# Feed-forward blocks of 2, 2, 4, 4, 4 token tiles instead of 2, 3, 4, 4, 3, and groups of six chunk pairs in the blocks of two

## Chip, cores, metric

The kernel runs on one core of a Trainium2 chip. The metric is the device time in microseconds (us). The engines are PE (TensorE, matmuls), PEld (its weight loads), DVE (VectorE), ACT (ScalarE), POOL (GpSimd) and SP (which issues the DMAs).

## The reference

One transformer layer on 2048 tokens of width 576: a conditioned layer norm, linear attention with 32 heads whose feature maps are softmaxes, a residual, a second conditioned layer norm, and a feed-forward of width 4608, all in bf16. What matters here is the end:

```python
h = _layernorm(x) * (1 + ca) + sa
x = x + ga * attention(h)                 # q, k, v, feature maps, numerator / denominator, @ wo
h = _layernorm(x) * (1 + cb) + sb
x = x + gb * (relu(h @ w1) @ w2)          # w1: 576 x 4608, w2: 4608 x 576
```

## The kernel before

The 16 tiles of 128 tokens go through the feed-forward in blocks. A block's first layer keeps its tokens as the moving operand (`nn` = 128 columns for each tile in the block) and w1 as the weights. There are 36 chunks of 128 hidden units. The input has 576 rows = 4 x 128 + 64, so each chunk takes four full matmuls and one "half chunk" of 64 rows; chunks j and j + 18 make a pair, whose two half chunks sit in the upper and lower 64 rows of the array and run at the same time. Chunk pairs are taken in groups: the group's first pairs get their full matmuls, then all pairs of the group get their half chunks, then the later pairs get their full ones. A matmul writes to a PSUM bank (512 fp32 columns); there are eight: four `psf`, `num0` to `num2`, and `pt`.

While block b is on PE, the next block's tiles are prepared in between: the softmax numerator of attention (`num`, made from phi, the feature map of q), its transpose, the output projection (`wo_tile`, with residual and statistics), the normalised xn, and xn's transpose into `h2T`. In block 0 the transposes are PE's; later they go through HBM by DMA. `put(us, f)` gives the point of the block, in us of feed-forward work, at which a step is emitted.

```python
FB = [(0, 2), (2, 3), (5, 4), (9, 4), (13, 3)]          # first tile, tiles
QREST = (2, 4, 8, 12, 16)                               # when phi of tiles 3..7 is made, in block 0
...
def ffn(b, steps):
    per = 512 // nn                                     # 2 for two tiles: two chunks share a bank
    def full(j, hps, last): ...                         # 4 matmuls of 128 rows for each of j, j + 18
    def rest(j, hps, last): ...                         # 1 matmul of 64 rows for each of j, j + 18
    size = 4
    for j0 in range(0, NJ // 2, size):
        js = list(range(j0, min(j0 + size, NJ // 2)))
        early, later = js[:len(js) // 2], js[len(js) // 2:]
        for j in early:
            pace(8 * nn / 2400)                         # emits the steps that are due
            bank[j] = bank[j - 1] if per > 1 and j - 1 in bank else [psf(), psf()]
            full(j, part(j), False)
        ...                                             # banks for the later pairs
        for j in js:
            rest(j, part(j), j in early)
        ...                                             # relu(early); full and relu for each later pair
    for tt in range(nt): ...                            # second layer: 72 matmuls of 288 columns a tile
...
total = FB[b][1] * (18 * 9 * P / 2400 + 72 * 0.12)      # 17.3 us for each tile of block b
lead, hop = (20, 12) if by_dma else (LEAD0, 8.3)        # by_dma = b > 0, LEAD0 = 11
gap = min(7.5 if b else GAP0, (total - lead) / nt)      # GAP0 = 5, nt = tiles of block b + 1
us0 = total - lead - gap * nt                           # tile i: num at us0 + gap*i, wo_tile hop later
```

The softmax here doesn't subtract the row's maximum and nothing guards it: scores larger than these inputs give would overflow.

## Time and profile before

| | before |
|---|---|
| time, median of the first 6 runs | 415.93 us (414.54 to 417.58) |
| profiled span | 414.7 us |
| PE busy | 98% |
| feed-forward part, first matmul of block 0 to the end | 89.72 to 414.69: 324.97 us |

From the page of the kernel before: span, PE's row, the granted clock in tenths over 40 slices, and the chain that ended last by engine and by line.

```profile
span 414.7 us, 8210 instructions
...
PE 405.8 (98%) x3447; PEld 284.2 (69%) x3459; DVE 224.8 (54%) x523; ACT 136.7 (33%) x305; POOL 61.8 (15%) x76
...
PEclk9999999999999999999999999999999999999999
...
PE 91%; DVE 4%; DMA 2%; ACT 1%; issue 1%; POOLq 0%; SPq 0%; ACTq 0%
PE psf L941 32%; PE psf L880 18%; PE two L484 10%; PE psf L484 4%; PE pt L880 3%; PE psf L887 3%; DVE R_sb L520 1%; PE kvacc L546 1%; DMA rW_60<-in_A_wqkv_dram 1%; DMA ph_66<-q_hbm 1%; DVE st L387 1%; PE two L680 1%; PE one L312 1%; DMA q_hbm<-Eq 1%; DVE mv L432 0%
```

PE has work nearly all the time, the clock is full, and the chain is 91% PE. So the time is the length of PE's stream, and a change can only win by shortening that stream or closing its holes.

The timeline of PE in the kernel before: start, length, engine, line, operation, operands, count. L880 is a full matmul, L887 a half chunk, L941 the second layer. The first rows are a group of block 0 (256 columns), the last two the step from block 1 to block 2.

```profile
92.36 0.61 PE L887 MATMUL psf<-h2T,rW_59 64*128 64x256 bf16 x8
92.90 3.67 PE L880 MATMUL psf<-h2T,rW_59 128*128 128x256 bf16 x32
96.50 0.61 PE L887 MATMUL psf<-h2T,rW_59 64*128 64x256 bf16 x8
97.04 3.67 PE L880 MATMUL psf<-h2T,rW_59 128*128 128x256 bf16 x32
...
193.89 1.27 PE L941 MATMUL psf<-rR_65,rH_1610 128*128 128x288 bf16 x9
194.99 3.62 PE L880 MATMUL psf<-h2T,rW_59 128*128 128x512 bf16 x15
```

Read start to start: from 92.90 to 96.50 there are 32 full matmuls in 3.60 us, which is 32 steps of 109 ns and about 0.1 more. From 96.50 to 97.04 eight half chunks in four pairs take 0.54 us, which is four steps of 109 ns and again 0.1 more. The extra stands at the two changes of mode: in the trace's own start times the last full matmul before a half chunk is about 95 ns longer than the others, and the last half chunk before a full one 92 ns. This is the same at 384 columns (258 and 255 ns for 163) and at 512 (312 and 308 for 216). In the last two rows (nine matmuls of 122 ns from 193.89), block 2 follows block 1 without a hole.

The preparation chain of block 2 in the kernel before: SP's timeline (a store of xn to HBM, then the transposing load of h2T), then DVE's (xn of the last tile, then the scaling of h2T).

```profile
182.64 0.33 SPq L835 DMA_DIRECT2D xn_hbm_2416<-xn  x1
184.58 2.70 SPq L840 DMA_TRANSPOSE h2T<-xn_hbm_2416  x1
```

```profile
181.98 0.63 DVE L445 TENSOR_SCALAR xn<-x_sb,rs 128x64 bf16<-128x64 bf16 x2
...
189.35 1.70 DVE L842 TENSOR_SCALAR h2T<-h2T,mod_76 128x512 bf16<-128x512 bf16 x5 [2.02 <-DMA h2T<-xn_hbm_2416]
```

The load is issued at 184.58, the scaling starts 4.77 us later and is over at 191.05. PE needs h2T at 194.99: 4 us of slack.

### The profile page before, as it was taken

The page shows a single profiled execution, that of the slowest core. Times are in us where ns is not written, and L with a number is a line of the kernel's source. Part 1 is how long each engine was busy: PE and PEld are TensorE (multiplying, and loading weights), DVE is VectorE, ACT ScalarE, POOL GpSimd, SP SyncE. Part 2 cuts the span into 40 slices and gives each one's busy share as a digit, 9 for nine tenths or more (in the row PEclk, how much of TensorE's full clock was granted, in tenths as well). Part 3 has the DMA queues.
Part 4 walks back from the last instruction along what each step waited for, and adds up shares of the span by engine and source line. Part 5 has one row for each costly group of instructions (what it writes and reads, how often), then busy time and mean ns, then how long its engine had stood idle before and what let it go on. Part 6 is the DMA issues. An engine that isn't in the chain of part 4 may idle for free.

```text
span 414.7 us, 8210 instructions
## 1 busy us (share of the span) xinstructions
PE 405.8 (98%) x3447; PEld 284.2 (69%) x3459; DVE 224.8 (54%) x523; ACT 136.7 (33%) x305; POOL 61.8 (15%) x76
## 2 busy tenths in 40 slices
PE   8999999989999999999999999999999999999997
PEld 5777888858887565877444588774446778655776
DVE  3599999666755466443445674433445544333122
ACT  4488987575511343000344300002443000123000
POOL 6245466413200010000010110000111000000000
PEclk9999999999999999999999999999999999999999
DMA  8998973987530123112023343120022413000001
GB/s 228 210 230 180 358 264 161 269 318 217 148 81 16 43 64 95 48 45 66 14 58 89 87 123 63 50 70 5 10 77 61 136 47 78 16 1 2 2 14 31
DMA packets 67986, 42.21 MB, mean 102 GB/s; under 512 B 47980, under 2 KB 65260, under 8 KB 67436
## 3 DMA queue, kind: packets, MB, share of 16 engines
q1 hardware_dynamic: 67328, 41.66, 36.6%
q8 instruction: 27, 0.44, 0.4%
q10 hardware_dynamic: 620, 0.02, 0.1%
q14 instruction: 11, 0.09, 0.1%
HBM read 19.63 MB, written 10.68 MB: 73 GB/s over the span
## 4 chain that ended last, share of the span: by engine, by line
PE 91%; DVE 4%; DMA 2%; ACT 1%; issue 1%; POOLq 0%; SPq 0%; ACTq 0%
PE psf L941 32%; PE psf L880 18%; PE two L484 10%; PE psf L484 4%; PE pt L880 3%; PE psf L887 3%; DVE R_sb L520 1%; PE kvacc L546 1%; DMA rW_60<-in_A_wqkv_dram 1%; DMA ph_66<-q_hbm 1%; DVE st L387 1%; PE two L680 1%; PE one L312 1%; DMA q_hbm<-Eq 1%; DVE mv L432 0%
## 5 line engine op out<-in xcount | busy, mean ns | idle before, releaser
L941 PEld LDWEIGHTS <-rH_1610 128*128 128x128 bf16 x1188 | 113.2, 98 | 27.1
L941 PE MATMUL psf<-rW_60,rH_1610 128*128 128x288 bf16 (+2 forms) x891 | 113.2, 282 | 0.0
L880 PEld LDWEIGHTS <-rW_59 128*128 128x128 bf16 x720 | 68.1, 98 | 56.0 <-issue 8.1
L880 PE MATMUL psf<-h2T,rW_59 128*128 128x384 bf16 (+2 forms) x454 | 81.4, 327 | 1.1 <-ACT x_sb L323 0.4
L897 ACT ACTIVATE rH_1610<-psf 128x512 bf16<-128x512 f32 (+2 forms) x60 | 30.1, 545 | 106.5 <-PE psf L887 101.6
L535 POOL TENSOR_TENSOR Eq<-Eq,R_sb 128x576 bf16<-128x576 bf16 (+1 forms) x16 | 18.4, 1150 | 218.9 <-DVE R_sb L530 199.5
L946 DVE TENSOR_TENSOR rYT<-psf,gb_row 128x288 f32<-128x288 f32 (+2 forms) x33 | 14.7, 445 | 55.0 <-PE psf L941 54.9
L484 PEld LDWEIGHTS <-hTr 128*128 128x128 bf16 x360 | 34.2, 98 | 10.4 <-issue 1.1
L941 PE MATMUL psf<-rR_65,rH_1610 128*128 128x288 bf16 (+2 forms) x297 | 41.4, 282 | 0.0
L899 DVE TENSOR_SCALAR rH_1610<-psf 128x384 bf16<-128x384 f32 (+1 forms) x40 | 23.5, 616 | 29.8 <-PE psf L887 27.8
L520 DVE TENSOR_REDUCE R_sb<-Eq 128x64 f32<-128x1152 bf16 x16 | 21.6, 1348 | 21.3 <-ACT Eq L505 13.6
L484 PE MATMUL two<-rW_60,hTr 128*128 128x288 bf16 x240 | 31.9, 286 | 0.0
L958 POOL TENSOR_TENSOR rH_61<-rH_61,R_sb 128x1152 bf16<-128x1152 bf16 (+4 forms) x16 | 27.6, 1725 | 15.5 <-ACT R_sb L524 13.3
L391 ACT ACTIVATE rs<-mv,eps_t 128x1 f32<-128x1 f32 x14 | 4.1, 295 | 76.2 <-DVE mv L388 76.2
L495 ACT ACTIVATE rH_61<-two,rs 128x576 bf16<-128x576 f32 x32 | 22.0, 737 | 2.6 <-PE two L680 2.0
L818 DVE TENSOR_TENSOR x_sb<-x_sb,psf 128x288 bf16<-128x288 bf16 x28 | 12.2, 445 | 19.0 <-PE psf L484 18.9
L387 DVE BATCH_NORM_STATS2 st<-x_sb 128x6 f32<-128x288 bf16 x52 | 22.0, 447 | 0.7
L520 DVE TENSOR_REDUCE R_sb<-rH_61 128x64 f32<-128x1152 bf16 x16 | 21.4, 1340 | 0.0
L484 PE MATMUL psf<-wo_sb,oT 128*128 128x288 bf16 x140 | 19.4, 286 | 0.1
L484 PEld LDWEIGHTS <-oT 128*128 128x128 bf16 x160 | 15.6, 98 | 4.3 <-issue 0.3
L899 DVE TENSOR_SCALAR rH_1610<-pt 128x384 bf16<-128x384 f32 (+1 forms) x16 | 9.9, 621 | 12.7 <-PE pt L880 12.7
L947 DVE TENSOR_TENSOR x_sb<-rYT,x_sb 128x288 bf16<-128x288 f32 (+2 forms) x33 | 14.8, 448 | 1.0
(436 smaller groups left out, 449.9 us busy)
## 6 DMA issues: line engine op xcount, KB each, us to landing
rW_59<-in_B_w_dram SPq DMA_DIRECT2D x4, 1152.0 KB, 10.1
q_hbm<-Eq SPq DMA_DIRECT2D x16, 288.0 KB, 2.1
rW_60<-in_B_w_dram SPq DMA_DIRECT2D x3, 1296.0 KB, 10.2
out_dram<-x_sb SPq DMA_DIRECT2D x15, 144.0 KB, 1.8
o_hbm<-o_sb SPq DMA_DIRECT2D x11, 160.0 KB, 1.8
rW_60<-in_w_mod_dram SPq DMA_DIRECT2D x3, 576.0 KB
rR_65<-in_B_w_dram SPq DMA_DIRECT2D x1, 1296.0 KB, 6.8
rW_59<-in_w_mod_dram SPq DMA_DIRECT2D x4, 288.0 KB, 3.5
```

Source lines behind the costliest of these rows:

```text
L387: nc.vector.bn_stats(out=s[:, hf, :], in_=x_sb[:, t, hf * HD2:(hf + 1) * HD2])
L484: nc.tensor.matmul(ps(bk)[:, 0:cn], lhsT=lhs(ci), rhs=rhs[:, ci, c0:c0 + cn], start=(first and ci == CO[0]), stop=(ci == CO[-1]))
L495: nc.scalar.activation(out=E[:, :, sgn, :].rearrange("p (b h) e -> p b h e", b=2), in_=ps[:, :, 0:HD2].rearrange("p b (h e) -> p b h e", e ...
L520: nc.vector.tensor_reduce(out=R[:, 0, :], in_=flat.rearrange("p (n e) -> p n e", e=DH), axis=AXX, op=ALU.add)
L535: eng.tensor_tensor(out=e, in0=e, in1=R[:, 1, h0:h1].unsqueeze(2).to_broadcast([P, h1 - h0, DH]), op=ALU.mult)
L880: nc.tensor.matmul(ps, lhsT=w1a[:, ci, jj * P:(jj + 1) * P], rhs=hb[:, ci, :], start=(not last and ci == 0 and first(j)), stop=(last and c ...
L897: nc.scalar.activation(out=o, in_=i_, func=ACT.Relu)
L899: nc.vector.tensor_relu(o, i_)
L941: nc.tensor.matmul(ps[:, 0:cn], lhsT=H1[:, j, tt * P:(tt + 1) * P], rhs=w2q[j // 9][:, j % 9, c0:c0 + cn], start=(j == 0), stop=(j == NJ - 1))
L946: nc.vector.tensor_tensor(out=y, in0=ps[:, 0:cn], in1=gb_row[:, c0:c0 + cn], op=ALU.mult)
L947: nc.vector.tensor_tensor(out=x_sb[:, t, c0:c0 + cn], in0=y, in1=x_sb[:, t, c0:c0 + cn], op=ALU.add)
L958: eng.tensor_tensor(out=e, in0=e, in1=R[:, 1, n0:n1].unsqueeze(2).to_broadcast([P, n1 - n0, DH]), op=ALU.mult)
```

## The change

Its intent: fuller PSUM banks and fewer groups. The blocks become 2, 2, 4, 4, 4 tiles. In blocks of two tiles, six chunk pairs (three pairs of banks) form a group, so the half chunks of twelve chunks stand end to end, and there are three groups instead of five (4, 4, 4, 4, 2 pairs). The times of the q work in block 0 move too.

```diff
-QREST = (2, 4, 8, 12, 16)
+QREST = (2, 6, 9.5, 15, 20)
-    FB = [(0, 2), (2, 3), (5, 4), (9, 4), (13, 3)]
+    FB = [(0, 2), (2, 2), (4, 4), (8, 4), (12, 4)]
...
-        size = 4
+        size = 6 if per > 1 else 4
-            early, later = js[:len(js) // 2], js[len(js) // 2:]
+            early, later = js[:2 if per > 1 else len(js) // 2], js[2 if per > 1 else len(js) // 2:]
...
-                if few:
-                    bank[j] = bank[j - 1] if per > 1 and i else [psf(), psf()]
+                if per > 1:
+                    bank[j] = bank[j - 1] if i % 2 else [pn.tile([P, 512], FP32, name="num2"), one_b()] if i == 0 else [psf(), psf()]
+                elif few:
+                    bank[j] = [psf(), psf()]
...
-                    pace(10 * nn / 2400, few)
+                    pace(10 * nn / 2400, few and (per == 1 or j > later[1]))
...
-                steps.append((us, lambda: f(*args), f in (num_tile, q_tile)))
+                steps.append((us, lambda: f(*args), f in ((num_tile, q_tile) if FB[b][1] > 2 else (tr_tile,))))
...
-                    put(QREST[i], q_rest, t, max(0, int(QREST[i] / 0.97) - 2))
+                    put(QREST[i], q_rest, t, min(NJ // 2 - 1, max(0, int(QREST[i] / 0.97) - 2)))
```

More of the change, by code (lines that the diff above doesn't have):

```diff
@@ L872, in first @@
         def first(j):
-            return per == 1 or j % 2 == 0 or j == NJ // 2 - 1
+            return per == 1 or j % 2 == 0
         def full(j, hps, last):
@@ L908, in part @@
             def part(j):
-                m = (j % 2) * nn if per > 1 and len(js) == 4 else 0
+                m = (j % 2) * nn if per > 1 else 0
                 return [ps[:, m:m + nn] for ps in bank[j]]
@@ L925, in ffn @@
                 rest(j, part(j), j in early)
-            group = lambda l: [l] if per > 1 else [[j] for j in l]
+            group = lambda l: [l[i:i + 2] for i in range(0, len(l), 2)] if per > 1 else [[j] for j in l]
             for g in group(early):
```

## The prediction

> **What bounds the kernel now.** TensorE's stream of matmuls. The page gives PE busy 98%, granted clock 1.00, and the chain that ended last as 91% PE. In the timeline of PE the feed-forward part (89.7 us to the end) has hardly a hole: start to start, matmuls of 256, 288, 384 and 512 columns take 109, 122, 163 and 216 ns, which is N/2.4 plus about 2.5 ns[...]. Beyond that I find in that part only:
> - 25 passes through the half chunks of rows (64-row matmuls, two at once). Each costs about 95 ns going in and 92 ns coming out, whatever the width: 0.19 us a pass, 4.7 us in all. The Trainium skill (TensorEngine Tiling, Key Properties) says that changing the tiling mode drains TensorE; the trace agrees.
> - some five short waits (for PSUM banks or phi), about 1 us in all, and 0.8 us at the start of the first block.
>
> **What the change does.**
> 1. Widths 256, 384, 512, 512, 384 become 256, 256, 512, 512, 512. There are still five blocks with the same number of matmuls, and the sum of columns is the same. As the cost is linear in N, this is worth 0.
> 2. Blocks of two tiles take three groups of six chunk pairs instead of five of four (the last of two). Passes: 25 become 3+3+5+5+5 = 21, so 4 x 0.19 = -0.75 us, all on the critical path.
> 3. Block 1 has two tiles instead of three, so one tile fewer is prepared by PE transposes during block 0: five transposes of o (0.27 us) and five of xn (0.27 us) go to DMA: -0.5 us.
> 4. New pressure: block 1 (two tiles, 35 us of feed-forward) must now prepare four tiles; the gap is 3.6 us a tile instead of 7.5. The last output projection stands about 12.5 us of feed-forward before the block's end (before: 15.5). From the trace: projection start to h2T ready = 4.3 (residual, statistics, xn) + 1.9 (store) + 4.8 (transposing DMA) + 1.7 (scale) = 12.7 us, against 1.2 + 12.5 = 13.7 us available. It just fits, with 1 us of slack where before had 4. In block 1's first layer DVE is nearly full (9 relus of 0.65, four softmax ratios of 1.4, two residual chains of 3.1): I allow 0.3 to 1 us of PE waits for PSUM banks there.
> 5. The later blocks of four have the pattern that block 2 has now, which shows no stall above 0.25 us. The tail is unchanged.
>
> Sum: -0.75 - 0.5 + about 0.4 = -0.9 us.
>
> **Prediction: 415.0 us, range 413.0 to 417.2. Faster by over 2%: 0.01; within 2%: 0.96; slower by over 2%: 0.03.**
>
> **What would show each step.** (1) The same start-to-start times, 109 and 216 ns. (2) 21 runs of 64-row matmuls; in blocks 0 and 1 three of 12, with 0.19 us of extra each. (3) 10 transposes of o and 10 of xn on PE after block 0 starts, from 15 and 15. (4) PE waiting for h2T at the start of block 2 would mean that the chain did not fit; waits on psf in block 1, bank pressure.
>
> **What would make it wrong.** The DMA chain of four tiles falling behind (two o buffers, three xn buffers), and block 2 starting late: slower by 2 to 6 us. Or six-pair groups waiting for relu before the shared banks come free in every group: up to 1 us each.

## The result

The changed kernel took 415.19 us (median of 20 runs, 413.13 to 416.11), the kernel before 416.4 us in the same rounds (40 runs). The ratio is 0.9971, 95% interval 0.9956 to 0.9985. Ratios here and below are the mean time of one kernel's fast runs over the mean of the other's fast runs of the same rounds, so not quite the ratio of the medians quoted.

From the page of the changed kernel, the same lines:

```profile
span 413.9 us, 8176 instructions
...
PE 404.3 (98%) x3433; PEld 284.3 (69%) x3449; DVE 223.1 (54%) x514; ACT 134.4 (32%) x293; POOL 61.8 (15%) x76
...
PEclk9999999999999999999999999999999999999999
...
PE 94%; DVE 3%; DMA 1%; ACT 1%; issue 0%; SPq 0%; ACTq 0%
PE psf L943 34%; PE psf L880 17%; PE two L484 10%; PE psf L484 4%; PE pt L880 4%; PE psf L887 3%; PE kvacc L546 1%; DMA rW_60<-in_A_wqkv_dram 1%; DVE R_sb L520 1%; DVE st L387 1%; PE two L680 1%; PE one L312 1%; DVE mv L432 0%; DVE rW_60 L382 0%; PE one L281 0%
```

The timeline of PE in the changed kernel: a group of block 0 with its twelve half chunks (the rows left out are four on `num` and `pt`), and the step from block 1 to block 2.

```profile
92.56 0.39 PE L887 MATMUL psf<-h2T,rW_59 64*128 64x256 bf16 x4
...
93.01 0.38 PE L887 MATMUL psf<-h2T,rW_59 64*128 64x256 bf16 x4
93.33 0.61 PE L880 MATMUL num_1629<-h2T,rW_59 128*128 128x256 bf16 x4
...
172.26 1.27 PE L943 MATMUL psf<-rR_65,rH_1610 128*128 128x288 bf16 x9
173.51 2.86 PE L880 MATMUL psf<-h2T,rW_59 128*128 128x512 bf16 x10
```

The twelve half chunks run from 92.56 to 93.33: 0.77 us, which is six pairs of 109 ns and 0.11 more (the other 0.09 is ahead of them). So the change of mode still costs the same 0.19 us, but once for twelve and not for eight. The last row is new: from 173.51, the first four matmuls of block 2 stand 323 ns apart in the trace, not 216, and 173.51 itself is 0.145 us late. PE lost 0.145 + 3 x 0.107 = 0.47 us there. (My expectations below say 0.57: I had counted one step too many, beside a matmul whose record is missing.)

The preparation chain of block 2 in the changed kernel, SP and DVE:

```profile
159.06 5.23 SPq L835 DMA_DIRECT2D xn_hbm_2380<-xn  x2
166.66 2.76 SPq L840 DMA_TRANSPOSE h2T<-xn_hbm_2380  x1
```

```profile
163.29 0.64 DVE L445 TENSOR_SCALAR xn<-x_sb,rs 128x64 bf16<-128x64 bf16 x2
...
173.05 1.70 DVE L842 TENSOR_SCALAR h2T<-h2T,mod_76 128x512 bf16<-128x512 bf16 x5 [3.43 <-DMA h2T<-xn_hbm_2380]
```

The last store is issued at 163.96 (second of the two that the first row merges), and the load only 2.70 us later (1.93 before). The scaling starts 6.39 us after the load's issue (4.77 before). PE then takes each piece of h2T as DVE delivers it, which is the 323 ns.

Because the part ahead of the feed-forward is the same program in both and yet ends anywhere from 87.9 to 89.9 us in the profiles below, I compare the feed-forward parts, block by block (from the first full matmul of a block to that of the next, PE timeline):

| profile | block 0 | 1 | 2 | 3 | 4 | sum | runs of half chunks | half clock near 90 us |
|---|---|---|---|---|---|---|---|---|
| before | 43.66 | 61.61 | 82.61 | 80.05 | 57.04 | 324.97 | 25 | no |
| changed | 41.46 | 42.13 | 82.93 | 82.60 | 74.82 | 323.94 | 21 | no |
| a1_after | 43.04 | 41.99 | 82.77 | 82.61 | 74.79 | 325.20 | 21 | yes |
| e1_lead | 41.45 | 41.99 | 82.61 | 82.61 | 74.81 | 323.47 | 21 | no |
| e2_groups4 | 41.88 | 43.30 | 82.93 | 82.60 | 74.82 | 325.53 | 25 | no |
| e3_pairs | 43.03 | 41.99 | 84.10 | 83.98 | 75.65 | 328.75 | 33 | yes |
| e4_blocks_old | 45.02 | 61.62 | 82.61 | 80.10 | 57.02 | 326.37 | 23 | no |
| e5_qrest_old | 62.53 | 41.99 | 82.91 | 82.61 | 74.81 | 344.84 | 21 | no (later, see there) |
| e6_featdma | 42.44 | 41.99 | 82.61 | 83.74 | 74.59 | 325.37 | 21 | yes |
| e7_shift | 42.61 | 41.99 | 82.63 | 82.60 | 74.79 | 324.62 | 21 | yes |
| e8_lead_fill | 41.28 | 42.03 | 82.61 | 82.60 | 74.80 | 323.32 | 21 | no |
| e9_featdma_fill | 40.72 | 42.12 | 82.61 | 82.61 | 74.59 | 322.65 | 21 | no (by its 109 ns steps; the clock record is empty) |
| e10_before_fill | 44.18 | 61.61 | 82.61 | 83.69 | 57.03 | 329.12 | 25 | no |

Before to changed is -1.03 us. The start times account for it: four runs of half chunks fewer, 4 x 0.188 = -0.75; ten PE transposes of 56 ns fewer (five of o, five of xn), -0.56; two short waits that went (0.15 and 0.27 us in blocks 1 and 3 of before), -0.42; the late h2T, +0.47; and the stretch from the start of the last matmul to the end, which is 3.13 us before and 3.46 in the changed kernel, +0.32. (It is 3.43 to 3.46 in the other kernels with the new blocks, but 3.23 in e6 and e9. The matmuls and the last store do not make it: from the last landing of that store to the end, where only event semaphores of the program's end are left, it is 0.87 us before and 1.15 in the changed kernel.) That makes -0.94; 0.1 us is not placed. Four gaps of 0.22 us, one each in blocks 2 and 3 of both traces, are no waits: a matmul's record is missing there, seven of eight being recorded. The prediction's "five short waits, about 1 us" must count such gaps, as the trace of before has only the two waits after the start of block 0.

### The profile page after: what moved, and what is told of

Same layout as the page of the kernel before. It is cut to its first block, busy times and chain, and to the rows that moved or that the text cites. A ratio compares the mean times of both kernels' runs of the same rounds, so it can differ in the third digit from the quotient of the medians.

```text
span 413.9 us, 8176 instructions
## 1 busy us (share of the span) xinstructions
PE 404.3 (98%) x3433; PEld 284.3 (69%) x3449; DVE 223.1 (54%) x514; ACT 134.4 (32%) x293; POOL 61.8 (15%) x76
## 4 chain that ended last, share of the span: by engine, by line
PE 94%; DVE 3%; DMA 1%; ACT 1%; issue 0%; SPq 0%; ACTq 0%
PE psf L943 34%; PE psf L880 17%; PE two L484 10%; PE psf L484 4%; PE pt L880 4%; PE psf L887 3%; PE kvacc L546 1%; DMA rW_60<-in_A_wqkv_dram 1%; DVE R_sb L520 1%; DVE st L387 1%; PE two L680 1%; PE one L312 1%; DVE mv L432 0%; DVE rW_60 L382 0%; PE one L281 0%
## 5 line engine op out<-in xcount | busy, mean ns | idle before, releaser
L880 PE MATMUL psf<-h2T,rW_59 128*128 128x512 bf16 (+1 forms) x420 | 77.5, 330 | 1.2 <-ACT x_sb L323 0.4
L897 ACT ACTIVATE rH_1610<-psf 128x512 bf16<-128x512 f32 x48 | 26.7, 595 | 104.6 <-PE psf L887 97.3
L899 DVE TENSOR_SCALAR rH_1610<-psf 128x512 bf16<-128x512 f32 x36 | 23.7, 681 | 27.6 <-PE psf L887 24.5
L880 PE MATMUL pt<-h2T,rW_59 128*128 128x256 bf16 (+1 forms) x96 | 19.5, 326 | 0.0
L899 DVE TENSOR_SCALAR rH_1610<-pt 128x512 bf16<-128x512 f32 x15 | 10.4, 691 | 15.2 <-PE pt L880 15.2
```

The source lines that it names most:

```text
L880: nc.tensor.matmul(ps, lhsT=w1a[:, ci, jj * P:(jj + 1) * P], rhs=hb[:, ci, :], start=(not last and ci == 0 and first(j)), stop=(last and c ...
L897: nc.scalar.activation(out=o, in_=i_, func=ACT.Relu)
L899: nc.vector.tensor_relu(o, i_)
```

## The experiments

Each was checked against the reference and timed against the kernel before on the same chip. The interval of a ratio from six runs is about 0.3% (1.2 us), wider than most of what is asked. Two theories of the late h2T stand against each other: F, an instruction fetch holds up the load; S, four tiles in a two-tile block do not fit.

### a1_after: the changed kernel again

No edit.

> The changed kernel once more, so that the variants stand beside it on one chip. All theories: ratio to the kernel before 0.996 to 0.9985 again. The question it answers is the start of block 2: in the first profile TensorE lost 0.57 us there, fed by the scaling of h2T chunk by chunk, and the two last DMAs of that chain took 2.6 us (store of xn) and 6.4 us (transposing load) where the kernel before shows 1.8 and 4.7; each overlapped an instruction-fetch packet (8 KB and 16 KB, 0.7 and 1.1 us) and one straggling stream of packets ended 0.6 and 1.4 us after the others. Theory F (the fetch is the cause): if the fetches fall at the same place again the same loss of 0.4 to 0.8 us appears; if they fall elsewhere, the load takes 4.7 us and the loss is 0 to 0.2. Theory S (the four tiles in 35 us simply do not fit): the loss is 0.5 us or more wherever the fetches fall.

Measured: 415.34 us, ratio 0.9962 (0.9934 to 0.9990). The fetches fell at the same place, and the load again took 6.38 us to the scaling; the wait at the start of block 2 was about 0.2 us. This agrees with F and does not exclude S. It also brought something unasked: block 0 took 43.04 us, 1.58 more. The stretches of this profile (busy time and count of each engine, then the granted clock, the DMA share and GB/s):

```profile
core 0: us, PE busy (x) PEld busy (x) DVE busy (x) ACT busy (x) POOL busy (x), PEclk, DMA share, GB/s
86.00:90.00 4.00, 2.52 (x22) 1.54 (x21) 3.23 (x12) 3.50 (x8) 0.64 (x1) 1.00 1.09 392
90.00:94.00 4.00, 3.64 (x25) 2.19 (x23) 0.00 (x0) 0.89 (x3) 0.00 (x0) 0.59 0.25 95
94.00:98.00 4.00, 4.00 (x38) 3.47 (x37) 1.90 (x3) 2.21 (x6) 1.35 (x2) 0.98 0.89 220
```

In the second stretch the mean clock is 0.59. The trace's clock record has half clock from 90.7 us for 3.4 us, beginning 81.9 us after the clock was first released.

### e1_lead: more lead in block 1

```diff
-            lead, hop = (20, 12) if by_dma else (LEAD0, 8.3)
+            lead, hop = (22 if b == 1 else 20, 12) if by_dma else (LEAD0, 8.3)
```

> The changed kernel with the preparation in block 1 started so that the last projection stands 1.5 us earlier (gap 3.14 us a tile instead of 3.64). Theory chain-late (TensorE waits at the start of block 2 because the chain projection, xn, store, transposing load, scale ends too late): the wait of 0.57 us at the start of block 2 is gone, first matmuls of block 2 start 216 ns apart, time 0.3 to 0.6 us below the changed kernel (ratio to before about 0.9957), if tighter spacing costs no new PSUM wait. Rival (the wait is for PSUM banks, or for the relus of block 1): the wait stays at 0.5 us or more and the time is the same as the changed kernel's.

Measured: 414.21 us, ratio 0.9946 (0.9915 to 0.9978). Blocks 1 and 2 are 41.99 and 82.61 us, the matmuls at the start of block 2 stand 216 ns apart, and no new wait came. DVE of this profile:

```profile
168.57 1.70 DVE L842 TENSOR_SCALAR h2T<-h2T,mod 128x512 bf16<-128x512 bf16 x5 [4.72 <-DMA h2T<-xn_hbm]
```

The scaling starts 2.95 us ahead of block 2's first matmul (171.52). So it was the chain's lateness that PE waited for, not banks. (This load was not held up, as the table under e7_shift shows: 4.92 us to its last completion. That the longer lead also takes a late load is seen in e8_lead_fill.) The gain on the trace is 0.47 us; on the clock it is not resolved against a1_after.

### e2_groups4: new blocks, old groups

```diff
-        size = 6 if per > 1 else 4
+        size = 4
```
and the other lines about groups and banks as in the kernel before.

> The new blocks (2, 2, 4, 4, 4) with the old groups of four pairs in the blocks of two tiles. Theory passes (each run of 64-row matmuls costs 0.19 us for going in and coming out): 25 runs in the trace instead of 21, and 0.75 us more in blocks 0 and 1 together than in the changed kernel; ratio to before about 0.9988 (0.9975 to 1.0005). Rival (the gain comes from the fuller relus and from the blocks themselves, the groups do nothing): same time as the changed kernel within 0.2 us, 0.997.

Measured: 416.26 us, ratio 0.9997 (0.9960 to 1.0034). PE in block 0:

```profile
92.54 0.61 PE L887 MATMUL psf<-h2T,rW 64*128 64x256 bf16 x8
93.08 3.67 PE L880 MATMUL psf<-h2T,rW 128*128 128x256 bf16 x32
96.68 0.61 PE L887 MATMUL psf<-h2T,rW 64*128 64x256 bf16 x8
97.22 1.05 PE L880 MATMUL psf<-h2T,rW 128*128 128x256 bf16 x8
```

Eight half chunks at a time again, 25 runs. Blocks 0 and 1 together are 85.18 us, 83.59 in the changed kernel: +1.59, twice the expected 0.75. Block 0, where nothing else differs, gives 0.42 for two runs (0.38 expected). Block 1 has besides a wait of 0.42 us (start times) of an output projection for `psf`, and PE waits 0.33 us more at its end for h2T. So the runs cost what was claimed, and the six-pair groups save a bank wait that I had not seen. In e2 the projection stands right behind the half chunks and waits for the relu of a `psf` bank; in the changed kernel it stands behind the full matmuls on `num2` and `pt` (half chunks over at 148.55, projection at 150.31), and by then the relu is done.

### e4_blocks_old: old blocks, new groups

```diff
-    FB = [(0, 2), (2, 2), (4, 4), (8, 4), (12, 4)]
+    FB = [(0, 2), (2, 3), (5, 4), (9, 4), (13, 3)]
-QREST = (2, 6, 9.5, 15, 20)
+QREST = (2, 4, 8, 12, 16)
```

> The old blocks (2, 3, 4, 4, 3) and old times of the q work, with the new groups of six pairs, which then touch block 0 alone. Theory passes: 23 runs of 64-row matmuls, block 0 shorter by 0.38 us, ratio to before about 0.9991 (0.998 to 1.0). Ten transposes of o and xn more than in the changed kernel, and no wait at the start of block 2. Rival (six-pair groups bring waits for banks): block 0 the same or longer than before.

Measured: 416.65 us, ratio 1.0003 (0.9975 to 1.0030). Two runs fewer, yet block 0 is 1.36 us longer than before. The expectation was wrong, and the rival nearer. PE's waits in block 0, who waited for whom, in total, times, longest:

```profile
PE num L769 <- DMA ph<-q_hbm: 0.8, 1, 0.8
PE pt L792 <- ACT rH L897: 0.7, 1, 0.7
```

Three tiles to prepare put the steps 5 us earlier than two do. The transpose of o then falls into the first layer and needs the bank `pt`, which the six-pair groups now use, so it waits for the relu of that bank; and the numerator of tile 3 comes before its phi has landed (it was due at 103.87 us; in the kernel before, with the same times but four-pair groups, it stands at 106.59). In start times these are 0.90 and 0.89 us, and -0.38 + 1.79 = +1.41 against 1.36 measured. The groups pay only together with the smaller block 1, which moves both steps past the first layer.

### e7_shift: instruction fetches moved

```diff
     spin(5)
+    spin(64, 1)          # 64 matmuls of one column while PE waits for its first data
     turn_m(1)
```

> The changed kernel with 64 matmuls of one column (128 instructions of TensorE with their weight loads) put in at its very start, where TensorE waits for its first data. They only move the places in time at which TensorE's 16 KB instruction fetches fall, by half of the distance between two. In the three traces so far with the same instruction stream in block 1 (both of the changed kernel, and the old groups) 15 of the 16 completions of the transposing load of block 2 came by 4.8 us and the sixteenth at 6.4 us, just behind such a fetch (4.1 to 5.2 us after the issue). Theory F (the fetch holds up one of the 16 DMA engines and with it the load): no fetch between 3.5 and 5 us after the issue, all 16 completions by 4.9 us, the wait of TensorE at the start of block 2 is at most 0.2 us (0.57 and 0.31 before). Rival S (the load is slow for another reason at that place, such as the output store beside it): 6.4 us again and the wait stays. Time from the first matmul of block 0 to the end 323.5 us if no throttled stretch falls in (323.94 in the changed kernel's first profile); total the same as the changed kernel within 1 us, as the start may come some tenths later.

Measured: 417.41 us, ratio 1.0025 (1.0000 to 1.0051). The scaling of h2T starts 4.79 us after the load's issue and blocks 1 and 2 are 41.99 and 82.63 us: the wait is gone, with the lead unchanged. DMA of the changed kernel in a window of block 1's end (packets, MB, share; then issues with size and time to landing), then that of this kernel:

```profile
q8 instruction: 1, 0.02, 0.6%
q14 instruction: 1, 0.01, 0.4%
...
h2T<-xn_hbm_2380 SPq DMA_TRANSPOSE x1, 6.4
```

```profile
q14 instruction: 1, 0.01, 0.3%
...
h2T<-xn_hbm SPq DMA_TRANSPOSE x1, 4.8
```

No q8 fetch, and a load of 4.8 instead of 6.4 us. The records of the load's 16 completions, us after its issue, in eight loads of several profiles:

```
profile, load of block   15th    16th    q8 fetch of 16 KB, from - to
before, 2                4.74    4.75    none
changed, 2               4.80    6.36    4.07 - 5.19
a1_after, 2              4.88    6.35    4.30 - 5.30
e2_groups4, 2            4.80    6.33    4.10 - 5.23
changed, 4               4.63    6.10    3.86 - 5.02
a1_after, 4              4.70    4.71    3.90 - 5.07
e1_lead, 2               4.89    4.92    4.21 - 5.42
e7_shift, 2              4.74    4.76    none
```

Fifteen completions are in time and one is 1.4 to 1.6 us late, in four loads, each beside a fetch of 16 KB; but four loads had all 16 in time, two of those beside a fetch. These eight are a choice. All 13 profiles together hold 41 such loads of h2T. In 17 of them a 16 KB fetch was in flight in the last part (later than 2 us after the issue): ten of these had one completion 1.4 to 1.6 us late, seven lost 0.12 us at most. Of the 24 others none lost more than 0.05 us. So in these traces the loss needs a fetch, but a fetch does not always bring it, and what decides stays open. A fetch is one packet of 16 KB, 0.9 to 2.3 us long; the kernel before has 27 of them for 6906 matmuls and weight loads, one for 256, so they should be PE's instructions. If such a packet goes through one DMA engine, only the load's part on that engine would be late, which fits the one late completion. The Trainium skill (DMA: Bandwidth & Descriptors, Queues, rings and completion order) says that each engine goes round its queues packet by packet; the traces agree as far as they go, but they do not name the engine of a packet, so that it was the same engine is inferred. S is refuted: with the old lead the chain fits when no fetch meets it, by 0.5 us (scaling over at 173.88, block 2 at 174.40).

The total was worse than I expected by 2 us, and that is not explained in full. All six runs have the clock of 0.996, that is the half-clock stretch of a1_after, against nine of 21 for the changed kernel; block 0 is 1.15 us longer for it. Why the rest of the start is slower was not followed.

### e3_pairs: more runs of half chunks

```diff
-        size = 6 if per > 1 else 4
+        size = 6 if per > 1 else 2
```

> The changed kernel with groups of two pairs instead of four in the three blocks of four tiles: nine runs of 64-row matmuls a block instead of five, 33 in all instead of 21. Theory passes (0.188 us a run whatever its length): the blocks of four are 0.75 us longer each, 2.26 us in all, ratio to before about 1.0024 (1.001 to 1.004); if it is more, the trace must show waits for PSUM banks beside it. Rival (a run costs by its number of matmuls or the trace's start times mislead): the time stays at that of the changed kernel, 0.997.

Measured: 418.65 us, ratio 1.0049 (1.0012 to 1.0085): slower than the kernel before, by less than 1%. PE in the last block, where no other work is mixed in:

```profile
343.49 0.60 PE L887 MATMUL psf<-h2T,rW 64*128 64x512 bf16 x4
344.03 3.63 PE L880 MATMUL psf<-h2T,rW 128*128 128x512 bf16 x16
347.59 0.61 PE L887 MATMUL psf<-h2T,rW 64*128 64x512 bf16 x4
348.13 3.63 PE L880 MATMUL psf<-h2T,rW 128*128 128x512 bf16 x16
```

Sixteen full and four half matmuls take 347.59 - 343.49 = 4.10 us; at 216 ns for each of 18 slots it would be 3.89. So 0.21 us a group, and block 4 is 0.83 us longer for four groups more. Blocks 2 and 3 are 1.5 and 1.4 us longer than in e1_lead: 0.83 for the runs and one wait each of 0.53 us (start times) of an output projection for `psf`, as the expectation allowed. This is the amplified form of e2's test, and it shows on the clock too.

### e5_qrest_old: old times of the q work

```diff
-QREST = (2, 6, 9.5, 15, 20)
+QREST = (2, 4, 8, 12, 16)
```

> The changed kernel with the old times of the q work (2, 4, 8, 12, 16). There are four phi buffers after the first two tiles; with the new blocks the softmax numerators of tiles 2 and 3 are at 13.6 and 18.6 us, so the phi of tiles 6 and 7, put at 12 and 16 us, would be written in program order into the buffers of tiles 2 and 3 before these are read. Expected: a WRONG result on purpose (tiles 2 and 3), at about the same time. Rival (the new times of the q work are a tuning for speed, not needed): correct, and slower by over 0.5 us.

Measured: correct, 436.35 us in one run of unknown state. Both halves of the expectation failed. PE's waits in block 0:

```profile
PE num L769 <- DMA ph<-q_hbm: 17.7, 2, 11.0
```

Block 0 is 62.5 us long, 41.46 in the changed kernel; the numerators of tiles 2 and 3 wait 17.7 us for phi and the clock is halved twice behind these waits. So the numerators wait for a phi that is written late, as they would if they waited for tiles 6 and 7. Why the result passed (whether the right phi was read, or the comparison does not see two tiles' phi) stays open. In either case the new times are not a fine tuning; without them the new blocks lose 20 us.

### e6_featdma: xn of block 1 transposed by DMA as well

```diff
-            lead, hop = (20, 12) if by_dma else (LEAD0, 8.3)
+            lead, hop = (22 if b == 1 else 20, 12) if by_dma else (LEAD0 + 2, 8.3)
-                if by_dma:
+                if True:
                     put(us + hop + 0.1, xn_out, b + 1, t0 + i)
-            if by_dma:
+            if True:
                 put(total - 6, feat_dma, b + 1)
```

> The changed kernel with the longer lead in block 1 (as in e1_lead) and with the features of block 1 transposed by DMA instead of TensorE in block 0, which starts that preparation 2 us earlier. Theory (TensorE's stream is all that counts): ten transposes of xn fewer, 0.55 us, so block 0 is 40.9 us long instead of 41.45, the feed-forward part about 322.9 us, ratio to before about 0.994 to 0.995. Rival (the chain through HBM does not fit into block 0, which also carries the q work and the last weights on the same queue): TensorE waits at the start of block 1 or for phi of tile 3 in block 0, and block 0 is not shorter than 41.45 us.

Measured: 414.53 us, ratio 0.9959 (0.9929 to 0.9989). Block 0 was 42.44 us, with the half-clock stretch in it, so this profile alone could not tell. Block 3 lost 1.1 us:

```profile
PE num L769 <- DMA ph<-q_hbm: 1.0, 1, 1.0
```

The store ahead of that phi had 15 completions by 2.05 us and the sixteenth at 4.28, with a 16 KB fetch from 301.79 to 303.33 us on the way (store issued at 300.61). In e1_lead the same store's sixteenth came at 2.73. This is F's pattern at another place.

### e10_before_fill, e8_lead_fill, e9_featdma_fill: holes ahead of block 0 filled

Half clock near 90 us stands in four of the first ten profiles (a1, e3, e6, e7); the five that the expectation below speaks of counted the half clock of e5, which has another origin.

```diff
-    ... Qm6 J1a J1b Je1a:v
+    ... Qm6 HT5 J1a J1b HT1 Je1a:v
+        elif name == "HT":
+            fill = acc()                                  # a PSUM bank pair that is free here
+            for i in range(n):
+                nc.tensor.matmul(fill[:, 0, :], lhsT=ident[:, :], rhs=wo_sb[:, 0, 0:512], start=True, stop=True)
```

> The kernel before with six dummy matmuls of 512 columns (results never read) in the holes that TensorE has just before block 0, five while it waits for xn of tile 1 and one while it waits for h2T. In five of the ten profiles so far a stretch of half clock begins 81.9 us after the clock was released, 3.4 us long, and costs 1.4 to 1.6 us at the start of block 0; in the others there is none. Theory H (the holes make a slice of low activity, and where the slices of 3.4 us happen to fall on it the clock is halved for the next one): with the holes filled no half-clock stretch begins near 90 us in any run, the runs with a mean clock of 0.996 vanish, and the median falls by about half of 1.5 us, ratio to before 0.997 to 0.9995. Rival (the stretch has another cause): the 0.996 runs stay and the ratio is 0.999 to 1.001.

> The changed kernel with the longer lead (e1_lead) and the dummy matmuls. Theory: block lengths as in e1_lead (41.45, 41.99, 82.6, 82.6, 74.8 us), feed-forward 323.5 us in every profile, no half-clock stretch near 90 us; ratio to before 0.992 to 0.9945. Rival (the fill does nothing): 0.9946 to 0.997, with some runs at a clock of 0.996.

> e6_featdma with the dummy matmuls. In e6_featdma block 0 was 42.44 us long, of which a half-clock stretch took about 1.5, and block 3 lost 1.1 us to a wait for phi whose store had its sixteenth completion at 4.3 us instead of 2.0, beside a 16 KB fetch. Theory: block 0 about 40.9 us without the stretch; the six dummies move the fetches by 12 instructions of 256, too little to clear block 3, so the wait of about 1 us there may stay: feed-forward 323 to 324 us with it, 322.8 without. Ratio to before 0.992 to 0.995, not clearly better than e8_lead_fill.

Measured: e10_before_fill 417.31 us, ratio 1.0008 (0.9984 to 1.0032); e8_lead_fill 413.64 us, 0.9923 (0.9900 to 0.9946); e9_featdma_fill 413.88 us, 0.9920 (0.9896 to 0.9944). The first stretches of e8_lead_fill:

```profile
86.00:90.00 4.00, 3.53 (x25) 1.79 (x23) 2.51 (x10) 3.54 (x7) 0.00 (x0) 1.00 1.07 389
90.00:94.00 4.00, 4.00 (x44) 3.23 (x42) 1.57 (x2) 1.77 (x4) 0.18 (x1) 1.00 0.34 84
```

PE is busy 3.53 of the first 4 us, 2.52 in a1_after, and the clock stays at 1.00. The kept traces show what decides. Count windows of 3.413 us from the first release of the clock. In a1, e3, e6 and e7 the window that ends at 89.6 to 90.7 us has PE busy for 47 to 57% of it (1.79 of 3.41 us in a1), and the half clock begins with its end. In e1 and e4 the window on these holes has 62% (2.11 us), in before, changed and e2 they fall into two windows of 71 to 74%, and no half clock follows. In e8 and e10 no window there is under 86%. So it is the place of the holes in the windows that decides, and in these traces the limit lies between 57 and 61% (the last is a window near the end of e8). Of the twelve runs of e8 and e9, eleven have a clock of 1.000 and one 0.999. For these two the theory held: block 0 is 41.28 and 40.72 us, and the sums are 323.32 and 322.65. In e8 the load of block 2 met a fetch again (6.43 us), and the longer lead took it.

For e10 the total went against the expectation. Its profile has no half clock near 90 us, but numerators wait for phi, in block 0 (0.5 us) and in block 3 (2.1 us). In block 0 the sixteenth completion of a store ahead of phi is 1.3 us late beside a 16 KB fetch; in block 3 twelve of the 16 completions of phi's load are late (the last at 5.61 us, 3.64 in the kernel before). A fetch ran there too, but this is not the pattern of one late completion, and its cause is not shown. A half-clock stretch follows at 330.6 us, behind a window with PE busy for 40%:

```profile
PE num L769 <- DMA ph<-q_hbm: 2.6, 2, 2.1
```

One of the seven runs has a clock of 0.996 and one 0.999. So filling removes the stretch at its place, but for the kernel before it brought no gain: its one profile lost as much to the waits for phi. Twelve instructions more do move the fetches, but that this is why the waits came, and that the two cancel in the unprofiled runs as well, is not shown.

## Why the prediction was right

Predicted were 415.0 us and -0.9 us; measured 415.19, and a ratio of 0.9971, which is -1.2 us, against -1.03 in the profiles.

1. Widths worth nothing: right. The steps are 109 and 216 ns in both kernels, and blocks 2 to 4 with full width are 82.6 and 74.8 us for four tiles as the sum of columns asks.
2. Runs of half chunks, -0.75: right. 21 runs, each 0.19 us; e2 (0.42 for two) and e3 (0.83 for four) confirm it from both sides.
3. Transposes moved to DMA, -0.5: right, ten and ten are left after block 0 starts. e9, which moves ten more, has block 0 shorter by a further 0.56 us than e8.
4. New pressure, +0.3 to +1.0, taken as +0.4: the place was right, the cause was not, and that the 0.47 us measured is near it is luck. The prediction put it at bank waits in block 1, and held that the chain to h2T "just fits, with 1 us of slack". The mis-sized term is that chain: 12.7 us predicted from the durations before, 159.65 to 174.75 = 15.1 us measured. Its store took 0.8 us and its load 1.6 us more, where instruction fetches met them. PE lost 0.47 us there, and no bank wait came in block 1. In the kernel before none of the three loads met a fetch in its last part, and with 4 us of slack it would not have shown.
5. Later blocks and tail unchanged: the blocks are right within 0.05 us apart from the late start (82.61 in e1_lead); the tail became 0.32 us longer, at the program's end. This and the two waits that went (-0.42) were not forecast and nearly cancel, so the closeness of the sum owes something to luck too.

What was missing: the prediction took the trace's durations as fixed. Between runs the same kernel moves by more than the whole gain. Of the 27 runs of the changed kernel (21 and the six of a1_after), the 13 with a clock of 0.996 took 415.55 us in the mean and the 14 with 0.999 or more 414.51: the half clock is worth about 1.0 us. But those 14 alone lie between 413.13 and 415.57. This second spread was not explained; in the profiles e1_lead reaches block 0 at 88.08 us and the changed kernel at 89.92, with the same program up to there.

## What to carry to other kernels

When PE is 98% busy, cost a change of blocking in PE start times: N/2.4 + 2.5 ns a matmul, 0.19 us for each excursion to 64-row matmuls, and the instructions that move to other engines; then look for bank waits, which made e2 and e4 come out otherwise than expected. Do not count on a DMA chain that "just fits": here a late completion, always beside an instruction fetch, held ten of 41 loads for 1.4 to 1.6 us, and 2 us more of lead took it. And look at holes ahead of a dense PE stream (here of 1.28, 0.20 and 0.35 us): where one window of 3.41 us had PE busy for 57% or less, the clock was halved for the next 3.4 us, and dummy matmuls in the holes prevented it, though for the kernel before that brought no gain in time.

## What the Trainium skill lacked or had wrong

- TensorE: Matmul & The Clock Gate, What's actually happening: half clock is said to come after an idle window of about 3.4 us. Here a window that was not idle was enough: PE was busy for 53% of it in a1_after (1.79 of 3.41 us), and for 47 to 57% in four profiles; windows with 61% and more were not followed by half clock. (Further down the page reports half clock from short idle times between groups of matmuls, but gives no such share.) The page's free-running window of 3413 ns agrees: the stretch was 3.4 us long and began 81.9 us, 24 times that, after the release in four profiles.
- TensorE: Matmul & The Clock Gate, Back-to-back issue gap: the page calls N/2.4 + 2.5 ns the isolated gap and gives about 131 ns for N = 512 in a real stream of weight loads and matmuls. Here that stream has 216 ns at 512 columns and 109 at 256; the formula held in the stream. (Higher up the same page measures 215.7 ns back to back at 512, as here.)
- TensorEngine Tiling, Key Properties: a change of tiling mode is said to drain TensorE, and no cost is given. Here it was 95 ns going in and 92 ns coming out, the same at 256, 384 and 512 columns.
- DMA: Bandwidth & Descriptors, Queues, rings and completion order: the page puts refill on row 14. Here instruction packets of 16 KB (27 in a run, 0.9 to 2.3 us each in the 13 profiles) came on q8 and packets of 8 KB on q14. No page says that a refill can delay a DMA: here ten of the 17 loads that a fetch met had a sixteenth completion 1.4 to 1.6 us behind the fifteenth, and a store one of 2.2 us (e6_featdma).
